# A long-attention and token-mixer kernel: the third batch is begun earlier, the v copies change engine, and TensorE gets more filler

## The chip, the cores and the metric

The kernel runs on one core of one Trainium2 chip, as one program. Five engines work beside each other, each taking its own instructions in order: TensorE (PE; its weight loads are shown as PEld), VectorE (DVE), ScalarE (ACT), GpSimd (POOL) and SyncE (SP), which does little but hand out DMA transfers. The metric is the device time of one execution in microseconds (us), the median of several. An execution's time contains the span from its first to its last instruction and a little around it.

## What is computed

Inputs are q, k and v of 8 batches, 8 heads, 576 positions and 64 dimensions, eight global positions, and four weight matrices. Attention is limited to a band of 32 positions on either side, except that the eight global positions see everything and are seen by everything. The attention output of the eight heads, side by side, is x (8 x 576 x 512). An MLP-mixer block follows, once over the positions and once over the channels:

```python
scores = scale * np.matmul(q, k.transpose(0, 1, 3, 2))
mask = (np.abs(pos[:, None] - pos[None, :]) <= 32) | is_global[:, None] | is_global[None, :]
attn = softmax(np.where(mask, scores, -1e9))
x = heads_side_by_side(np.matmul(attn, v))
u = x + (np.maximum(x.T @ w_tok1, 0.0) @ w_tok2).T
out = u + np.maximum(u @ w_ch1, 0.0) @ w_ch2
```

## The kernel before

The order of every instruction is written out by hand: an engine takes its instructions in the order in which the Python code emits them, and the framework only adds the semaphores. The work of one batch has short names in the code, which the whole text uses.

**Attention of batch b.** `load_qk` and `load_rest` (SP) fetch q and k as 32-bit numbers; `cast_qk` makes 16-bit copies, a pair of heads at a time (`casts` gives ten such steps: the rest rows and four pairs, for q and for k). `T(b, p)` turns one head pair with eight transposes on TensorE, and `TE` copies the two results on VectorE into `qT` and `kT`; `t` is both. `TR` does the same for the last 64 rows, with `TRE`. `globals_` copies the queries of the global positions into `qT` (L391). `S_(b, p, part)` computes half of a head pair's banded scores, and `SX` (ScalarE, L469) exponentiates them into `e_all`. `SM` (VectorE) picks the global queries' part into `eg` (L475) and multiplies `e_all` with the band's mask (L480). `GK` computes the scores of the global keys, with two exponentials and a mask product (`LM`, L531). `OG` (L538) multiplies `eg` with v and leaves `rf` (L543, VectorE). `PV(b, tau)` makes the output of 128 positions; VectorE divides (L677, L678) into `x16s`. `PV` needs v twice: as loaded by POOL's DMA queue (`load_v16`, five loads, into `vsh`), and shifted by 64 rows (`vod`), which `v_odd` makes with two copies of 64 x 2112 elements (L372, L373), on POOL for most batches.

**Mixer of batch b.** `M1` is the first token product (L691, five chunks, then one Relu on ScalarE, L695); `M2` the second (L711), whose sums VectorE makes (L716, L719); `M3` turns them by DMA transposes on SP's queue (L728) into `uT`. `M4(b, j)`, j from 0 to 11, is one group of the first channel product ("product 1", L739) with a Relu (L742), and `M5(b, tau, part)` half a tile of the second ("product 2", L765); after the second half VectorE adds (L769) and SP stores the tile (L770). `M4l` and the fifth tile of M5 handle the last 64 positions of two batches together, in odd b (L752, L772).

**How the two are woven.** `dense(b)` lists the units of M4 and M5 of batch b, 20 for even b and 25 for odd ones. While these run, attention of the next batches is put between them. For b=0, `period_0` is a hand-written list in which every `D` (None) stands for "the next dense unit"; `play` walks it and then emits the units that are left. For b=1, `merge` interleaves the list `sparse2()` with the dense units by the costs written beside the entries. From b=2 on, `first_half(b)` is played with product 1 and `second_half(b)` with product 2; there PV and the token product of batch b+1 and the turning and scoring of batch b+2 are placed. Since POOL has little else to do, its queue runs ahead of this order: a `load_v16` goes out as soon as the PV that last read its buffer is done.

The prologue (L883 to L1016) does the attention and token product of batch 0 by pairs of heads; `W(n)` (L205) puts n matmuls of 128 x 128 on TensorE whose result nobody reads. Its last POOL instructions load the weights, q, k and v of batch 1 and cast batch 1's q and k.

PSUM tiles come from three pools: `psS` with two slots (scores, most turned pairs, M1, M2), `psV` with one (PV of even tau, GK, OG) and `psM` with two (M4, M5, and the turned pairs of batches 0 and 2).

Of the kernel before, what the change touches and what calls it, by code (L numbers as in the profile page):

```python
# [44 lines left out]
def kernel(  # L45
# [156 lines left out]

    warm = psv([P, P], name="warm")

    def W(n):  # L205
        for _ in range(n):
            nc.tensor.matmul(warm, lhsT=ident, rhs=ident, start=True, stop=True)

    def indices():
        g16r = const.tile([1, NG], F16)  # L210
# [156 lines left out]
            nc.gpsimd.dma_start(out=dr.rearrange("p i d -> p (i d)"), in_=rest_src(ten, 1))  # L367
            nc.gpsimd.dma_start(out=dst.rearrange("p h i d -> p h (i d)"), in_=qk_src(ten, 1, slice(0, H)))

    def v_odd(b, hs=slice(0, H), eng=nc.gpsimd):  # L370
        i = b % 2
        eng.tensor_copy(out=vod[i][HQ:P, :, hs], in_=vsh[i][HQ:P, 0 : NT - 1, hs])  # L372
        eng.tensor_copy(out=vod[i][0:HQ, :, hs], in_=vsh[i][0:HQ, 1:NT, hs])  # L373
# [13 lines left out]
    def casts(b):  # L387
        return [lambda ti=ti, p=p: cast_qk(b, ti, p, nc.scalar.copy) for p in (None, 0, 1, 2, 3) for ti in range(2)]
# [53 lines left out]
    def S_(b, p, part):  # L442
        qf = qTs[b % 2][:, p].rearrange("p t x -> p (t x)")
        kT = kTs[b % 2][:, p]
        ps = pss([P, 2, 512], name=f"s{part}_{b}_{p}")
        a, z = ((0, 2 * QS), (2 * QS, ES))[part]
        if b == 0:
            for par in range(2):
                nc.tensor.matmul(ps[:, par, 0 : z - a], lhsT=ident, rhs=band[:, 0 : z - a], start=True, stop=False)
        js = ((0, 1, 2, 3, 4), (4, 5, 6, 7, 8, 9))[part]  # L450
        for j in js:
            i0 = max(qcol(j - 1), a)
            i1 = min(qcol(j) + HQ + NG * (j % 2 == 0), z)
            o = slice(HQ * (j % 2), HQ * (j % 2) + HQ)
            for par in range(2):
                r = slice(64 * par, 64 * par + 64)
                nc.tensor.matmul(  # L457
                    ps[o, par, i0 - a : i1 - a], lhsT=kT[r, HQ * j : HQ * j + HQ], rhs=qf[r, i0:i1],
                    start=b > 0, stop=b > 0 or j in js[-2:],
                )  # L460
        st[b]["s", p, part] = ps
        if b > 0:
            SX(b, p, part)
# [7 lines left out]
    def SM(b, p):  # L471
        e2 = e_all[:, 2 * p : 2 * p + 2]
        if b > 0:
            gc = bass.AP(tensor=e2.tensor, offset=e2.offset, ap=[e2.ap[0], [QS, NT], [ES, 2], [1, NG]])
            nc.vector.tensor_tensor(  # L475
                out=eg[:, :, 2 * p : 2 * p + 2, 0:NG], in0=gc, in1=egm.unsqueeze(2).to_broadcast([P, NT, 2, NG]), op=ALU.mult
            )
        bm = bandm.rearrange("p c x -> p (c x)")[:, 0:ES]
        for par in range(2):
            nc.vector.tensor_mul(out=e2[:, par], in0=e2[:, par], in1=bm)  # L480
# [26 lines left out]
    def GK(b):  # L507
        s = st[b]
        ps = (psv if b != 2 else pss)([P, 2, 512], name=f"gk_{b}")
        for p in range(NP):  # L510
            o = ps[32 * p : 32 * p + 32]
            qv = qTs[b % 2][:, p, :, NG:QS]
            w = kgz[:, b, p, :]
            nc.tensor.matmul(o[:, 0, 0:384], lhsT=w, rhs=qv[:, 0:3], start=True, stop=True)
            nc.tensor.matmul(o[:, 1, 0:128], lhsT=w, rhs=qv[:, 3], start=True, stop=True)
            nc.tensor.matmul(o[:, 1, 128:192], lhsT=w, rhs=qv[:, 4, 0:LAST], start=True, stop=True)
        s["gk"] = ps
        if b > 0:
            LX(b)
            LM(b)  # L520
# [255 lines left out]
    def t(b, p):  # L776
        T(b, p)
        TE(b, p)

    def sparse2():  # L780
        b, n = 2, 3
        cs = casts(n)

        def cast(k):
            return [(0.0, c) for c in cs[2 * k : 2 * k + 2]]

        u = [(0.0, lambda: (load_rest(n), load_qk(n, slice(0, H))))]
        for p in (2, 3):
            u += [(0.3, lambda p=p: S_(b, p, 0)), (1.8, lambda p=p: S_(b, p, 1)), (0.0, lambda p=p: SM(b, p))]
            if p == 2:  # L790
                u += [(0.3, lambda: GK(b))]
        u += [(2.5, lambda: OG(b))]
        u += [(2.0, lambda: PV(b, 0)), (2.0, lambda: PV(b, 1)), *cast(0), (2.0, lambda: PV(b, 2)), *cast(1)]
        u += [(0.0, lambda: PV(b, 3)), (1.0, lambda: [M1(b, ch) for ch in range(3)]), *cast(2)]
        u += [(2.0, lambda: PV(b, 4)), *cast(3), (3.0, lambda: [M1(b, ch) for ch in range(3, NT)]), *cast(4)]
        u += [(0.0, lambda: (load_rest(n + 1), load_qk(n + 1, slice(0, H))))]
        u += [(0.0, lambda: (load_v16(n), v_odd(n)))]
        u += [(1.3, lambda: (M2(b, 0), M3(b, 0))), (1.0, lambda: (M2(b, 1), M3(b, 1)))]
        u += [(2.0, lambda: (M2(b, 2), M3(b, 2) if b % 2 else None))]
        u += [(1.0, lambda: (globals_(n), TR(n)))]  # L800
        u += [(1.2, lambda p=p: t(n, p)) for p in range(NP)]
        for p in range(NP):
            u += [(0.3, lambda p=p: S_(n, p, 0)), (2.2, lambda p=p: S_(n, p, 1)), (0.0, lambda p=p: SM(n, p))]
            if p == 2:
                u += [(0.5, lambda: GK(n))]
        u += [(0.5, lambda: OG(n))]
        return u

# [13 lines left out]
    def period_0():  # L822
        n, m = 1, 2
        D = None
        c2 = casts(m)
        u = [D, D, D, D, D, lambda: TR(n), D, lambda: globals_(n), lambda: t(n, 0), D]
        u += [lambda: t(n, 1), D, s2(n, 0), D, lambda: t(n, 2), lambda: SM(n, 0), D, s2(n, 1), D, lambda: t(n, 3)]
        u += [lambda: SM(n, 1), s2(n, 2), D]
        u += [D, lambda: SM(n, 2), lambda: GK(n), s2(n, 3), D, lambda: SM(n, 3), D, D, D]
        u += [lambda: v_odd(n, eng=nc.vector), lambda: OG(n), D, lambda: (load_rest(m), load_qk(m, slice(0, H)))]  # L830
        u += [lambda: PV(n, 0), lambda: PV(n, 1), D, lambda: PV(n, 2), lambda: PV(n, 3), D]
        u += [lambda: PV(n, 4), lambda: [M1(n, ch) for ch in range(NT)], *c2]
        u += [lambda: (M2(n, 0), M3(n, 0)), lambda: (M2(n, 1), M3(n, 1)), lambda: globals_(m), lambda: TR(m), lambda: t(m, 0)]
        u += [lambda: (M2(n, 2), M3(n, 2)), lambda: (load_v16(m), v_odd(m)), lambda: t(m, 1), s2(m, 0), lambda: t(m, 2)]
        u += [lambda: SM(m, 0), lambda: t(m, 3), s2(m, 1), lambda: SM(m, 1)]
        return u

    def first_half(b):
        n, m = b + 1, b + 2
        D = None  # L840
        cs = casts(m) if m < B else []

        def c(k):
            return cs[2 * k : 2 * k + 2]

        def tt(p):
            return [lambda: t(m, p)] if m < B else []

        def pv(tau):
            return lambda: PV(n, tau)  # L850

        if n == B:
            return []
        u = [D, D, pv(0), D, pv(1), *c(0), D, pv(2), *c(1), D, pv(3), lambda: [M1(n, ch) for ch in range(3)], *c(2), D]
        if b == 2:
            u += [lambda: gather_t(1)]
        u += [pv(4), *([lambda: TR(m)] if m < B else []), *tt(0), *c(3), D, lambda: M1(n, 3), D, lambda: M1(n, 4), *c(4)]
        if m < B:
            u += [lambda: (load_v16(m), v_odd(m)), lambda: globals_(m)]
        if m + 1 < B:  # L860
            u += [lambda: (load_rest(m + 1), load_qk(m + 1, slice(0, H)))]
        u += [*tt(1), D, D, lambda: (M2(n, 0), M3(n, 0)), D, lambda: (M2(n, 1), M3(n, 1)), *tt(2), D]
        u += [lambda: (M2(n, 2), M3(n, 2) if n % 2 else None), D]
        return u

    def second_half(b):
        m = b + 2
        D = None
        if m >= B:
            return []  # L870
        return [D, s2(m, 0), D, lambda: t(m, 3), lambda: SM(m, 0), D, s2(m, 1), D, lambda: SM(m, 1), D, s2(m, 2), D,
                lambda: SM(m, 2), lambda: GK(m), s2(m, 3), D, lambda: SM(m, 3), D, lambda: OG(m)]

    def dense(b):
        u = [(0.86, lambda j=j: M4(b, j)) for j in range(NJ)]
# [34 lines left out]
    S_(0, 0, 0)  # L910
    TRE(0, (0,), A)
    TRE(0, (1,), V)
    S_(0, 1, 0)
    SX(0, 0, 0)
    G(out=g16[0][0], in_=g32[0][0])
    T(0, 2)
    load_w1()
    load_w1l()
    load_w2()
    SX(0, 1, 0)  # L920
    S_(0, 1, 1)
    TEk(0, 2, V)
    S_(0, 0, 1)
# [6 lines left out]
    G(out=g16[1][0], in_=g32[1][0])  # L930
    TEq(0, 3, A)
    TEk(0, 3, V)
    S_(0, 2, 0)
    castv(0)
    gather_t(0)
# [3 lines left out]
    castv(1)  # L939
    GKE(0)  # L940
    SX(0, 2, 1)
    GQ0()
    v_odd(0, slice(0, 2), nc.vector)
    v_odd(0, slice(2, 4), nc.vector)
    GK(0)
    GX0()
    S_(0, 3, 1)
# [3 lines left out]
    castv(2)  # L951
    load_wc1(0)
    SX(0, 3, 1)
    OG0(1)
    LM(0)
    OG0(0)
# [18 lines left out]
    load_v16(1)  # L975
    x_pads(1)
    qk_pads(1)
    for p in (None, 0, 1, 2, 3):
        cast_qk(1, 0, p, G)
        cast_qk(1, 1, p, G)  # L980
    gather(1)
# [76 lines left out]
```

The softmax here doesn't subtract the row's maximum and nothing guards it: scores larger than these inputs give would overflow.

## Time and profile before

| what | us |
|---|---|
| median of 7 runs | 354.27 |
| lowest and highest | 349.99, 355.27 |
| the profiled execution | 350.85 |
| its span, first to last instruction | 349.1 |
| TensorE busy | 311.4 (89% of the span) |
| VectorE busy | 189.5 (54%) |
| ScalarE busy | 153.6 (44%) |
| POOL busy | 86.7 (25%) |

Times of single instructions are from that one execution and count from the start of its span. In a timeline row stand the start, the duration, the engine, the line of the code, the operation, what it writes and reads, shape and count, and in brackets how long the engine was idle before and what ended that. "Granted clock" is the share of TensorE's full clock that the throttle let through: 1.00 or 0.50 in this trace, by stretches of 3.41 us or a multiple of it.

### The profile page before, as it was taken

How to read it: one execution, taken by the hardware profiler on the slowest of the kernel's cores; microseconds unless marked ns; L12 is line 12 of the kernel's file. 1: busy time of each engine (PE TensorE's matmuls, PEld its weight loads, DVE VectorE, ACT ScalarE, POOL GpSimd, SP SyncE). 2: the span in 40 equal slices, each digit the busy share in tenths (PEclk: the TensorE clock that was granted, in tenths of full speed). 3: DMA queues.
4: the chain of work that ended last, by engine and by line, in shares of the span. 5: the costliest groups of instructions: out<-in, count | busy, mean ns of one | idle time of the engine just before them, and what ended most of it. 6: DMA issues, size and time to landing. Idle time of an engine off the chain costs nothing.

```text
span 349.1 us, 8086 instructions
## 1 busy us (share of the span) xinstructions
PE 311.4 (89%) x3431; PEld 168.7 (48%) x3431; DVE 189.5 (54%) x395; ACT 153.6 (44%) x275; POOL 86.7 (25%) x111
## 2 busy tenths in 40 slices
PE   4599686984899989799989999899989999999993
PEld 4368343542446544454445645444545645444641
DVE  7488176845852766566656474565656364231021
ACT  2562435214858135653465453554455433413600
POOL 5948586441226000430044001520000000000000
PEclk9789989998999999999999999999999999999999
DMA  7999999199767972949294923959101221042012
GB/s 208 191 143 245 262 159 76 62 218 221 220 117 71 255 141 62 87 100 257 93 88 78 238 90 73 90 174 204 62 2 26 67 81 44 0 107 91 0 69 85
DMA packets 82023, 42.38 MB, mean 121 GB/s; under 512 B 56578, under 2 KB 76674, under 8 KB 81986
## 3 DMA queue, kind: packets, MB, share of 16 engines
q1 hardware_dynamic: 44080, 31.34, 33.7%
q0 software_dynamic: 37904, 10.52, 28.2%
q8 instruction: 27, 0.44, 0.5%
q14 instruction: 10, 0.08, 0.1%
q10 hardware_dynamic: 2, 0.00, 0.0%
HBM read 36.11 MB, written 9.44 MB: 130 GB/s over the span
## 4 chain that ended last, share of the span: by engine, by line
PE 72%; DMA 11%; issue 5%; DVE 5%; SPq 3%; POOL 2%; ACT 2%; ACTq 0%; POOLq 0%
PE op L765 25%; PE b1p L739 23%; DMA lk<-in_k_dram 9%; PE a1p L691 4%; PE s L457 4%; PE hp L711 4%; PE pT L399 3%; PE b1lp L752 3%; PE pv L655 3%; PE pv L664 2%; DMA lv<-in_v_dram 2%; DVE x L678 1%; PE og L538 1%; SPq L128 1%; SPq L126 1%
## 5 line engine op out<-in xcount | busy, mean ns | idle before, releaser
L742 ACT ACTIVATE b<-b1p 128x512 f16<-128x512 f32 x96 | 57.0, 598 | 91.5 <-PE b1p L739 89.6
L739 PE MATMUL b1p<-uT,wc 128*128 128x512 f16 x384 | 95.9, 383 | 0.5 <-ACT b L742 0.5
L765 PE MATMUL op<-wc,b 128*128 128x512 f16 x384 | 89.3, 380 | 0.0
L469 ACT ACTIVATE e_all<-s 128x544 f16<-128x544 f32 (+1 forms) x64 | 41.1, 685 | 41.2 <-issue 29.1
L360 POOL DMA_DIRECT2D vsh<-in_v_dram x35 | 29.6, 854 | 115.7 <-PE pv L664 99.2
L765 PEld LDWEIGHTS <-b 128*128 128x128 f16 x384 | 35.3, 98 | 39.4
L739 PEld LDWEIGHTS <-wc 128*128 128x128 f16 x384 | 34.6, 98 | 37.1 <-issue 1.8
L769 DVE TENSOR_TENSOR osb<-u,op 128x512 f32<-128x512 f16 x32 | 22.0, 688 | 53.9 <-PE op L765 51.7
L405 DVE COPY qT<-pT 128x512 f16<-128x512 f16 x30 | 20.6, 687 | 15.0 <-PE pT L399 11.3
L716 DVE TENSOR_TENSOR u<-x,hp 128x1024 f16<-128x1024 f16 x14 | 17.0, 1221 | 21.3 <-PE hp L711 21.3
L677 DVE RECIPROCAL rr<-pv 128x8 f32<-128x8 f32 (+1 forms) x35 | 7.2, 207 | 33.3 <-PE pv L664 33.2
L457 PE MATMUL s<-qT,kT 64*64 64x136 f16 (+2 forms) x704 | 18.6, 223 | 7.4 <-DVE kT L411 1.9
L480 DVE TENSOR_TENSOR e_all<-e_all,bandm 128x616 f16<-128x616 f16 x56 | 24.4, 476 | 1.0
L678 DVE TENSOR_TENSOR x<-pv,rr 128x512 f16<-128x512 f32 (+1 forms) x35 | 24.2, 691 | 1.2
L457 PEld LDWEIGHTS <-kT 64*64 64x64 f16 x704 | 11.9, 110 | 20.5 <-issue 13.6
L411 DVE COPY kT<-pT 128x512 f16<-128x512 f16 x30 | 20.4, 681 | 2.0 <-ACT qT L405 1.2
L399 PE MATMUL pT<-ident,qn 128*128 128x128 f16 x128 | 14.3, 242 | 7.2 <-DVE kT L437 6.3
L711 PE MATMUL hp<-a,w 128*128 128x512 f16 x72 | 18.9, 380 | 1.5 <-ACT a L695 1.5
L655 PE MATMUL pv<-rf,lf 128*64 128x264 f16 x126 | 18.9, 287 | 0.9 <-DVE kgz L354 0.7
L664 PE MATMUL pv<-vsh,e_all 128*64 128x66 f16 x280 | 18.5, 194 | 0.0
L664 PEld LDWEIGHTS <-e_all 128*64 128x64 f16 x504 | 18.4, 111 | 0.0
L385 ACT CAST qn<-lq 128x512 f16<-128x512 f32 x25 | 15.3, 613 | 6.5 <-DMA lq<-in_q_dram 6.5
(171 smaller groups left out, 368.6 us busy)
## 6 DMA issues: line engine op xcount, KB each, us to landing
out_dram<-osb SPq DMA_DIRECT2D x32, 256.0 KB
lq<-in_q_dram SPq DMA_DIRECT2D x6, 1024.0 KB
lk<-in_k_dram SPq DMA_DIRECT2D x6, 1024.0 KB
wc<-in_moe_w_ch_dram POOLq DMA_DIRECT2D x6, 512.0 KB
vsh<-in_v_dram POOLq DMA_DIRECT2D x21, 128.0 KB
vsh<-in_v_dram POOLq DMA_DIRECT2D x14, 96.0 KB
lq<-in_q_dram SPq DMA_DIRECT2D x4, 256.0 KB
lk<-in_k_dram SPq DMA_DIRECT2D x4, 256.0 KB
```

What stands on the lines that cost most here:

```text
L360: nc.gpsimd.dma_start(out=vsh[b % 2][r0:r1, c, :, 0:D], in_=v[b, :, j0 : j0 + (r1 - r0), :].rearrange("h p d -> p h d"),)
L399: nc.tensor.transpose(out=pT[:, ti, P * i : P * i + P], in_=n[b % 2][:, i, 2 * p : 2 * p + 2, :], identity=ident)
L457: nc.tensor.matmul(ps[o, par, i0 - a : i1 - a], lhsT=kT[r, HQ * j : HQ * j + HQ], rhs=qf[r, i0:i1], start=b > 0, stop=b > 0 or j in js[-2:],)
L469: nc.scalar.activation(out=e2[:, :, a:z], in_=ps[:, :, 0 : z - a], func=AF.Exp, scale=scale)
L480: nc.vector.tensor_mul(out=e2[:, par], in0=e2[:, par], in1=bm)
L655: nc.tensor.matmul(ps[r0 : r0 + 64, hf, 0 : NP * VW], lhsT=s["lf"][:, HQ * t : HQ * t + HQ], rhs=s["rf"][:, 2 * hf : 2 * hf + 2], start=Tr ...
L664: nc.tensor.matmul(ps[r0 : r0 + 64, hf, VW * hh : VW * hh + VW], lhsT=e_all[:, h, lo : lo + HQ], rhs=(vod if t % 2 else vsh)[b % 2][:, tau ...
L678: nc.vector.tensor_tensor(out=x16s[b % 2][r, tau, :].rearrange("p (f h x) -> p f h x", f=2, h=NP), in0=pq[r, :, :, 0:D], in1=rr[r].unsquee ...
L711: nc.tensor.matmul(ps[:, i, :], lhsT=w2[:, ch, P * tau - sh : P * tau - sh + P], rhs=s["a1"][:, ch, :], start=(ch == 0), stop=(ch == 1),)
L739: nc.tensor.matmul(ps, lhsT=wc1[:, cc, P * j : P * j + P], rhs=s["uT"][:, cc, :], start=(cc == 0), stop=(cc == 3))
L742: nc.scalar.activation(out=s["b1"][:, j, :], in_=ps, func=AF.Relu)
L765: nc.tensor.matmul(ps, lhsT=w, rhs=wc2[:, j, :], start=(j == 0), stop=(j == NJ - 1))
```

## The change

- `W` may take a fresh tile from `psM`. Seven calls with 74 matmuls together are added in the prologue: 30 before the scores of the second head pair, 12 before the turn of the third, five of 4 or 16 further on.
- POOL casts only the rest rows and pairs 0 and 1 of batch 1 in the prologue. Pairs 2 and 3 are cast by ScalarE in `period_0`.
- `period_0` is written anew: six instead of five dense units before `TR(1)`; the gk product of batch 1 and its last scores with a dense unit between; the loads of batch 2 after the 15th unit, ahead of `SM(1, 3)`; the v copies of batch 1 after that `SM`; the last unit before the last chunk of M1. Nine casts of batch 2 on ScalarE, and the tenth (pair 3 of k) on POOL, right before `load_v16(2)`. At the end the scores of batch 2's pair 2 with their `SM`, which were in `sparse2`.
- `sparse2` begins with `GK(2)` and pair 3, then the v copies.
- `v_odd` runs on VectorE for every batch. It leaves `period_0`'s tail and `first_half` and stands after `GK` in `sparse2` and `second_half`.

```diff
-    def W(n):
+    def W(n, fresh=False):
+        w = psm([P, P], name="warm2") if fresh else warm
         for _ in range(n):
-            nc.tensor.matmul(warm, lhsT=ident, rhs=ident, start=True, stop=True)
+            nc.tensor.matmul(w, lhsT=ident, rhs=ident, start=True, stop=True)
...
-    def v_odd(b, hs=slice(0, H), eng=nc.gpsimd):
+    def v_odd(b, hs=slice(0, H), eng=nc.vector):
...
         u = [(0.0, lambda: (load_rest(n), load_qk(n, slice(0, H))))]
-        for p in (2, 3):
-            u += [(0.3, lambda p=p: S_(b, p, 0)), (1.8, lambda p=p: S_(b, p, 1)), (0.0, lambda p=p: SM(b, p))]
-            if p == 2:
-                u += [(0.3, lambda: GK(b))]
+        u += [(0.3, lambda: GK(b)), (0.3, lambda: S_(b, 3, 0)), (1.8, lambda: S_(b, 3, 1)), (0.0, lambda: SM(b, 3))]
+        u += [(0.0, lambda: v_odd(b))]
         u += [(2.5, lambda: OG(b))]
...
-        u += [(0.0, lambda: (load_v16(n), v_odd(n)))]
+        u += [(0.0, lambda: load_v16(n))]
...
-                u += [(0.5, lambda: GK(n))]
+                u += [(0.5, lambda: GK(n)), (0.0, lambda: v_odd(n))]
...
-        c2 = casts(m)
-        u = [D, D, D, D, D, lambda: TR(n), D, lambda: globals_(n), lambda: t(n, 0), D]
-        u += [lambda: t(n, 1), D, s2(n, 0), D, lambda: t(n, 2), lambda: SM(n, 0), D, s2(n, 1), D, lambda: t(n, 3)]
-        u += [lambda: SM(n, 1), s2(n, 2), D]
-        u += [D, lambda: SM(n, 2), lambda: GK(n), s2(n, 3), D, lambda: SM(n, 3), D, D, D]
-        u += [lambda: v_odd(n, eng=nc.vector), lambda: OG(n), D, lambda: (load_rest(m), load_qk(m, slice(0, H)))]
+        c2 = casts(m)[:-1]
+        c1 = [lambda ti=ti, p=p: cast_qk(1, ti, p, nc.scalar.copy) for p in (2, 3) for ti in range(2)]
+        u = [D, D, D, D, D, D, lambda: TR(n), lambda: globals_(n), D, lambda: t(n, 0), *c1[:2], D]
+        u += [lambda: t(n, 1), *c1[2:], D, s2(n, 0), D, lambda: t(n, 2), lambda: SM(n, 0), D, s2(n, 1), D]
+        u += [lambda: t(n, 3), lambda: SM(n, 1), s2(n, 2), D, lambda: SM(n, 2), lambda: GK(n), D, s2(n, 3), D]
+        u += [lambda: (load_rest(m), load_qk(m, slice(0, H))), lambda: SM(n, 3), lambda: v_odd(n), D, lambda: OG(n), D]
         u += [lambda: PV(n, 0), lambda: PV(n, 1), D, lambda: PV(n, 2), lambda: PV(n, 3), D]
-        u += [lambda: PV(n, 4), lambda: [M1(n, ch) for ch in range(NT)], *c2]
+        u += [lambda: PV(n, 4), lambda: [M1(n, ch) for ch in range(NT - 1)], D, lambda: M1(n, NT - 1), *c2, D]
+        u += [lambda: (cast_qk(m, 1, 3, G), load_v16(m))]
         u += [lambda: (M2(n, 0), M3(n, 0)), lambda: (M2(n, 1), M3(n, 1)), lambda: globals_(m), lambda: TR(m), lambda: t(m, 0)]
-        u += [lambda: (M2(n, 2), M3(n, 2)), lambda: (load_v16(m), v_odd(m)), lambda: t(m, 1), s2(m, 0), lambda: t(m, 2)]
-        u += [lambda: SM(m, 0), lambda: t(m, 3), s2(m, 1), lambda: SM(m, 1)]
+        u += [lambda: (M2(n, 2), M3(n, 2)), lambda: t(m, 1), s2(m, 0), lambda: t(m, 2)]
+        u += [lambda: SM(m, 0), lambda: t(m, 3), s2(m, 1), lambda: SM(m, 1), s2(m, 2), lambda: SM(m, 2)]
...
-            u += [lambda: (load_v16(m), v_odd(m)), lambda: globals_(m)]
+            u += [lambda: load_v16(m), lambda: globals_(m)]
...
-                lambda: SM(m, 2), lambda: GK(m), s2(m, 3), D, lambda: SM(m, 3), D, lambda: OG(m)]
+                lambda: SM(m, 2), lambda: GK(m), lambda: v_odd(m), s2(m, 3), D, lambda: SM(m, 3), D, lambda: OG(m)]
...
     S_(0, 0, 0)
     TRE(0, (0,), A)
     TRE(0, (1,), V)
+    W(30)
     S_(0, 1, 0)
     SX(0, 0, 0)
     G(out=g16[0][0], in_=g32[0][0])
+    W(12)
     T(0, 2)
...
     SX(0, 3, 1)
+    W(16, True)
     OG0(1)
...
-    for p in (None, 0, 1, 2, 3):
+    for p in (None, 0, 1):
         cast_qk(1, 0, p, G)
         cast_qk(1, 1, p, G)
```

(Left out: four further calls of `W(4)`, before `S_(0, 1, 1)`, `S_(0, 2, 0)`, `GQ0()` and `GK(0)`.)

More of the change, by code (lines that the diff above doesn't have):

```diff
@@ L824, in period_0 @@
         D = None
-        c2 = casts(m)
-        u = [D, D, D, D, D, lambda: TR(n), D, lambda: globals_(n), lambda: t(n, 0), D]
-        u += [lambda: t(n, 1), D, s2(n, 0), D, lambda: t(n, 2), lambda: SM(n, 0), D, s2(n, 1), D, lambda: t(n, 3)]
-        u += [lambda: SM(n, 1), s2(n, 2), D]
-        u += [D, lambda: SM(n, 2), lambda: GK(n), s2(n, 3), D, lambda: SM(n, 3), D, D, D]
-        u += [lambda: v_odd(n, eng=nc.vector), lambda: OG(n), D, lambda: (load_rest(m), load_qk(m, slice(0, H)))]
+        c2 = casts(m)[:-1]
[4 more added lines that the diff above has]
+        u += [lambda: (load_rest(m), load_qk(m, slice(0, H))), lambda: SM(n, 3), lambda: v_odd(n), D, lambda: OG(n), D]
         u += [lambda: PV(n, 0), lambda: PV(n, 1), D, lambda: PV(n, 2), lambda: PV(n, 3), D]
-        u += [lambda: PV(n, 4), lambda: [M1(n, ch) for ch in range(NT)], *c2]
+        u += [lambda: PV(n, 4), lambda: [M1(n, ch) for ch in range(NT - 1)], D, lambda: M1(n, NT - 1), *c2, D]
+        u += [lambda: (cast_qk(m, 1, 3, G), load_v16(m))]
         u += [lambda: (M2(n, 0), M3(n, 0)), lambda: (M2(n, 1), M3(n, 1)), lambda: globals_(m), lambda: TR(m), lambda: t(m, 0)]
-        u += [lambda: (M2(n, 2), M3(n, 2)), lambda: (load_v16(m), v_odd(m)), lambda: t(m, 1), s2(m, 0), lambda: t(m, 2)]
-        u += [lambda: SM(m, 0), lambda: t(m, 3), s2(m, 1), lambda: SM(m, 1)]
+        u += [lambda: (M2(n, 2), M3(n, 2)), lambda: t(m, 1), s2(m, 0), lambda: t(m, 2)]
+        u += [lambda: SM(m, 0), lambda: t(m, 3), s2(m, 1), lambda: SM(m, 1), s2(m, 2), lambda: SM(m, 2)]
+        return u
         return u
@@ L920 @@
     SX(0, 1, 0)
+    W(4)
     S_(0, 1, 1)
@@ L932 @@
     TEk(0, 3, V)
+    W(4)
     S_(0, 2, 0)
@@ L941 @@
     SX(0, 2, 1)
+    W(4)
     GQ0()
@@ L944 @@
     v_odd(0, slice(2, 4), nc.vector)
+    W(4)
     GK(0)
```

## The prediction

> **What bounds the kernel now.** First the slices of the page, where every digit is the busy tenth of one fortieth of the span (8.7 us).
>
> ```profile
> PE   4599686984899989799989999899989999999993
> DVE  7488176845852766566656474565656364231021
> POOL 5948586441226000430044001520000000000000
> PEclk9789989998999999999999999999999999999999
> ```
>
> After about 95 us TensorE is full; what an edit can win lies in the first eleven slices. Second, the chain that ended last, for what paces those slices (start, us, what).
>
> ```profile
> 28.29 12.77 DMA lk<-in_k_dram
> 41.34 0.79 POOL vsh L360
> 42.17 0.52 POOL x L295
> ...
> 69.70 0.65 SPq L120
> 70.46 0.60 SPq L120
> 71.73 12.26 DMA lk<-in_k_dram
> 84.02 0.63 ACT kn L385
> ```
>
> Until 43 us the end hangs on batch 1's k and on POOL, not on TensorE. At 70 us it hangs on batch 2's k, which SP asks for only after an output store (L769, L770) has let it go. Third, the timeline of TensorE, whose brackets give each idle stretch.
>
> ```profile
> 43.09 0.32 PE L426 MATMUL pr<-ident,qr 128*64 128x64 f16 x8 [2.76 <-POOL qr L382]
> ...
> 55.17 0.34 PE L457 MATMUL s<-qT,kT 64*64 64x72 f16 x12 [1.94 <-DVE kT L411]
> ...
> 77.76 1.89 PE L711 MATMUL hp<-a,w 128*128 128x512 f16 x8 [1.48 <-ACT a L695]
> ...
> 84.69 0.40 PE L399 MATMUL pT<-ident,kn 128*128 128x128 f16 x4 [3.88 <-ACT kn L385]
> ```
>
> With the small ones (0.88, 0.79, 0.39, 0.28, 0.63, 0.47, 0.16) the idle time between 43 and 97 us is about 14 us. Fourth, VectorE beside POOL:
>
> ```profile
> 44.47 3.45 DVE L391 COPY qT<-gT 128x160 f16<-128x160 f16 x1
> ...
> 66.26 0.71 DVE L372 COPY vod<-vsh 64x2112 f16<-64x2112 f16 x1
> 67.00 0.70 DVE L373 COPY vod<-vsh 64x2112 f16<-64x2112 f16 x1
> ```
>
> The globals copy takes 0.20 us at 81.09, with POOL idle; here it ends just when POOL's casts do (47.86). The v copies of one batch cost VectorE 1.41 us; on POOL they took 1.94 and 2.06.
>
> **Prologue filler.** 74 more 128x128 matmuls. Twenty of them took 2.05 us of weight loads at 5.72, 0.103 each, so 7.6 us at half clock and, halving, an estimated 3.8 at full. 1.9 us fills the idle before the second head pair's scores (14.98). Nothing on POOL waits for TensorE there: its loads and casts keep their times, and the turn of batch 1's rest rows stays at 43.1. Against that TensorE has 2.76 us to spare, of which the sixth M4 group (0.86), now ahead of it, uses one part; 1.9 is left. Here the clock:
>
> ```profile
> 13.61:17.02 3.41, 2.04 (x28) 1.36 (x32) 1.71 (x4) 1.90 (x4) 3.41 (x7) 0.50 0.99 169
> 17.02:20.44 3.42, 3.42 (x49) 2.04 (x48) 2.21 (x5) 2.15 (x4) 0.69 (x2) 0.50 1.19 184
> 40.92:44.33 3.41, 1.21 (x19) 0.72 (x20) 0.54 (x2) 0.04 (x1) 2.95 (x6) 1.00 1.24 206
> 44.33:47.74 3.41, 3.41 (x18) 2.00 (x17) 3.41 (x2) 0.77 (x2) 3.41 (x7) 0.50 1.43 194
> ```
>
> The columns are stretch, length, busy us of PE, PEld, DVE, ACT, POOL, granted clock, DMA. A stretch 60% busy is followed by half clock when it was at half itself, one 35% busy by half clock. The Trainium skill (TensorE: Matmul & The Clock Gate, "Why this matters for your kernels") asks only that idle gaps stay below about 3 us. By that rule the 2.76 us gap costs nothing and this filler nothing but its price; by the rows it cost 3.4 us at half, in which 1.7 us of matmul time was lost. I go by the rows: 30 fillers make 13.61-17.02 full, so 17.02-20.44 runs at full, and wins back up to 1.7 of the 3.8; with ScalarE and VectorE now next there, TensorE reaches the M4 groups about 2 us later (bounds: 0.5 earlier to 4 later). All but 0.2 of it is inside the spare 1.9, and it leaves 40.92-44.33 over 70% busy, so the next stretch at full. **+0.2** (0 to 2.2).
>
> **Casts of batch 1.** Four of POOL's (0.56 pitch each) go to ScalarE, which stood idle 4.05 us there (ACT at 45.01): free. POOL's block then ends at 45.6, and L391 with it, so the first turn's copies start at 45.65 instead of 47.83. Walked on: second turn at 46.0, its copies to 48.2, where the second score part can start, against 50.36. The third pair's copies follow their turn (before they started at 53.83, 1.7 us after their turn's end, which no row of their own explains), so the 1.94 becomes 0.4; the 0.79 stays. Group thirteen starts at 54.4, where before group twelve started at 58.24: 3.84 plus its 0.87 is **-4.7** (the sixth group's move is in it). At half clock the same walk gives 55.7, -3.4.
>
> **v copies of batch 1** are on VectorE in both, but now come straight after SM(3) and ahead of rf: score end +1.4 (Exp) +1.1 (SM) +1.4 +0.7, and one store add 0.7, is 5.2, while TensorE comes to PV(0) at +4.3 to +4.6. **+0.6** (0 to 1.0). So M2 starts at 73.7, before 77.76.
>
> **Order inside product 2.** PV, OG, gk and M1 keep their durations; one M5 unit now stands before M1's last chunk, where before there was no wait (a gap of 0.15 or more is not in the timeline), so nothing. The list has 21 places for 20 dense units: the last, after the casts, stays empty, and the 1.48 before M2 with it.
>
> **Loads of batch 2** go out behind the first store, not the third: about 61 instead of 69.7. At the old 12.3 us k lands by 73 to 75, before ScalarE is through the token Relu; the POOL loads of v that shared the queues then (69.34 on) now come later. The last k pair's cast moves to POOL, idle then, which takes 0.5 off ScalarE's ten casts; they were not last in the tail. So the 3.88 and 0.39 go. Then VectorE is next: from M2's start, 1.06 to its first output, adds 2.35, globals and rest 1.0, that is to +4.2; the first pair's two copies to +5.4, ul's add +6.0, second pair +7.2, third +8.4, SM(0) +9.5, fourth pair +10.7, SM(1) and SM(2) to +12.9 (0.6 per copy, 1.1 per SM). Before, the first copy could start at +7.4 only. TensorE follows it: scores of pair 1 at +8.7, of pair 2 when ScalarE has freed their tiles, +9.5 to +10.4, gk to +11.6, and then the first M4 of batch 1; before that came at +12.75, with pair 2 and gk left over. uT's transposes, issued at +2.3 in four steps of 1.5, land near +10: no wait, if barely. Then two M4 instead of four before OG, one 0.7 wait for eg, the v copies ahead of rf: PV(0) of batch 2 at +17.7 with four M4 done; before +20.95 with six. 3.25 minus 2x0.87 is **-1.5** (-3 to +0.5).
>
> **v copies on VectorE** in each later batch (3 to 7). They sit between LM and SM(3), and eg, e_all, the store add, rf and OG queue behind. In the sparse stretch OG waits for eg already:
>
> ```profile
> 134.20 0.69 DVE L772 TENSOR_TENSOR osb<-ul,op 128x512 f32<-128x512 f16 x1 [0.55 <-PE op L765]
> 134.81 0.19 DVE L475 TENSOR_TENSOR eg<-e_all,egm 128x80 f16<-128x80 f16 x1
> ```
>
> The 0.55 idle before the store add, less the Exp rows that still come in it, hides 0.4 of the 1.41: OG comes 1.0 later. In the play-ordered periods eg was ready at 170.64 and OG started at 171.47; with the copies eg is ready at 171.74 (+0.3), and the store add, then rf, cost another 0.2 where no M5 follows: 2x0.5, and 2x0.25 in odd periods with their fifth tile. **+2.5** (0 to 7.0, all five uncovered). What comes back: L391 at 150.27 and 185.57 falls from 1.47 and 1.70 to 0.20. The Trainium skill (SBUF — State Buffer, "Who interferes with whom") says that copies on the port pair that VectorE and GpSimd share exclude each other for a whole instruction. By it alone the move gives VectorE about what it costs (1.3 against 1.41); but the idle row before TE at 151.99 shows nobody waiting for L391, so it gives the end nothing. I take nothing.
>
> **Sum.** 0.2-4.7+0.6-1.5+2.5 = -2.9 on the profiled execution: 349.1 span plus 1.75 around it, 350.85 to 348.0. That execution lies 3.4 below the median of its seven runs, which spread from 350 to 355. Nothing shown says why; I read it as throttled stretches that fall elsewhere in other runs, each worth up to 1.7, and let filler and denser units spare 1.0 of it, an estimate. 354.27-2.9-1.0 = **350.4**.
>
> **Rivals.** (1) Half clock stays at 44.33 and the copies lose another microsecond: the sum is -2.9+1.3+1.0, the spared 1.0 doesn't come: 353.7. For it: only 45% busy if the prologue doesn't slip. 0.38, nearly all within 1%.
> (2) Slower: batch 2's v comes too late. Its five loads, which POOL gave out at 52.89 before, now queue there behind the cast of the last k pair, and that waits for k. VectorE's v copy of batch 2 waits for them, with SM's successors, rf and every store add queued behind it, and OG reads the same rows. Alone the five took 7.7 us from first issue to landing (52.89 to 60.62); batch 3's, beside q and k traffic, took 16.5 (69.34 to 85.82). With k at 74 the first goes out at 74.7 and v lands between 82.4 and 91.2; the copies are due at 89.4 (M2's start +15.7). If batch 3's v, next in the same queue, and the transposes stretch it by another lone 7.7 it is 98.9: 9.5 us of stall, all of it on the path, 350.4+9.5 = 359.9. It turns the change into a loss once v lands after 93.3. Against it: q and k are asked for 8.7 us earlier into quiet queues. 0.14.
> (3) The whole 3.4 between median and profile goes with the throttled stretches, and the tail wins 3.0: 354.27-2.9-1.5-3.4 = 346.5. For it: two of the seven runs were without it already. 0.10.
> The forecast has 0.38.
>
> A measurement tells this kernel from no change at about 1% (3.5 us). Faster by more: all of (3) and 0.32 of the forecast, which lies just below that line with more room downwards (tail, filler), 0.42; slower 0.14; the rest 0.44. The range 346.0 to 357.0 takes in the bounds of tail and copies, and leaves out (2) and a little of (3).
>
> **To see afterwards.** L391 near 1.2 at 45 and 0.20 elsewhere; full clock from 20 to 48; SP's batch 2 loads near 61; no wait for kn L385 near 84, but waits for DVE in 74-90; OG behind eg by 0.3 to 1.0 from 134 on. Wrong if VectorE waits for vsh, if the turn of batch 1 moves past 44, or if each OG waits a full 1.4.

## The result, and the profile after

| what | before | after |
|---|---|---|
| median, us | 352.94 (62 runs) | 353.23 (25 runs) |
| lowest to highest | 348.60 to 358.14 | 350.23 to 356.75 |
| profiled span | 349.1 | 350.7 |
| granted clock over the span | 0.979 | 0.971 |

The ratio of after to before is 1.0049, with a 95% interval of 1.0024 to 1.0074: half a per cent slower, about 1.7 us, where 1.1% faster was forecast. Here and below a ratio compares runs on the same chip and leaves out the disturbed ones, which the medians contain, so the two can differ, in one case by 0.9%.

The slices of the changed kernel:

```profile
PE   5788998976799998799989999899989999999993
DVE  7477756849442866566655475565756384241021
POOL 5795640073031001300040001200000000000000
PEclk9989999996599999999999999999999999999998
```

TensorE is denser in slices 1, 2, 5 to 7 and 10 and thinner in 3, 4, 9 and 11, and POOL's busy time fell from 25% to 18% of the span. But the clock now has its dip in slices 10 and 11 (half clock from 81.5 to 95.2 us), deeper than any before. Next the timeline of TensorE, with the stalls that answer to those shown before. Line numbers are one higher than in the kernel before.

```profile
45.07 0.32 PE L427 MATMUL pr<-ident,qr 128*64 128x64 f16 x8
...
64.72 0.30 PE L656 MATMUL pv<-rf,lf 128*64 128x264 f16 x2 [0.60 <-DVE rf L544]
...
75.09 1.89 PE L712 MATMUL hp<-a,w 128*128 128x512 f16 x8 [1.17 <-ACT a L696]
...
90.04 1.87 PE L740 MATMUL b1p<-uT,wc 128*128 128x512 f16 x4 [3.29 <-DMA uT<-u]
...
134.94 0.46 PE L539 MATMUL og<-vsh,eg 128*32 128x132 f16 x17 [1.55 <-DVE eg L476]
```

The 2.76 and the 3.88 of before are gone. In their place stands a wait of 3.29 for uT, the transposed input of product 1 of batch 1. M2 of batch 1 comes 2.67 us earlier than before (75.09 against 77.76), but the first M4 group only 0.47 earlier (90.04 against 90.51), and its four matmuls take 1.87 instead of 1.04: half clock. The chain that ended last goes through the transposes:

```profile
80.51 0.70 DVE ul L720
81.21 0.27 SPq L729
81.48 0.05 issue
81.53 8.38 DMA uT<-u
89.91 0.14 issue
90.04 1.87 PE b1p L740 x4
```

The last of the four transposes is issued at 81.53 and lands 8.4 us later. What ran beside it is in POOL's timeline:

```profile
72.55 0.61 POOL L386 CAST kn<-lk 128x512 f16<-128x512 f32 x1 [22.32 <-DMA lk<-in_k_dram]
73.15 8.49 POOL L361 DMA_DIRECT2D vsh<-in_v_dram  x10
```

The cast of batch 2's last k pair held POOL's queue for 22 us. Behind it stood the v loads of batch 2, which had gone out at 52.89 before, and right after those went batch 3's: ten loads in one block, just where SP issues the transposes. In the 8.4 us from the last issue to the landing, 4399 packets of POOL's queue went through the DMA engines beside 2363 of SP's, and all but 64 of the 4399 before 87.0.

### The profile page after: what moved, and what is told of

Same layout as the page of the kernel before. It is cut to its first block, busy times and chain, and to the rows that moved or that the text cites. A ratio compares the mean times of both kernels' runs of the same rounds, so it can differ in the third digit from the quotient of the medians.

```text
span 350.7 us, 8246 instructions
## 1 busy us (share of the span) xinstructions
PE 317.0 (90%) x3505; PEld 172.8 (49%) x3505; DVE 193.8 (55%) x407; ACT 155.1 (44%) x278; POOL 61.4 (18%) x96
## 4 chain that ended last, share of the span: by engine, by line
PE 75%; DVE 16%; issue 4%; DMA 2%; ACT 1%; SPq 0%; DVEq 0%; ACTq 0%
PE b1p L740 24%; PE op L766 22%; PE a1p L692 5%; PE hp L712 4%; PE pv L656 3%; PE s L458 3%; PE b1lp L753 3%; PE pT L400 3%; PE pv L665 2%; DMA uT<-u 2%; DVE osb L770 1%; DVE vod L373 1%; DVE vod L374 1%; DVE qT L406 1%; DVE kT L412 1%
## 5 line engine op out<-in xcount | busy, mean ns | idle before, releaser
L770 DVE TENSOR_TENSOR osb<-u,op 128x512 f32<-128x512 f16 x32 | 21.9, 686 | 56.0 <-PE op L766 54.0
L400 PE MATMUL pT<-ident,qn 128*128 128x128 f16 x128 | 13.3, 230 | 8.7 <-DVE kT L438 7.4
L386 ACT CAST qn<-lq 128x512 f16<-128x512 f32 x27 | 16.5, 613 | 3.3 <-DMA lq<-in_q_dram 3.3
```

The source lines that it names most:

```text
L770: nc.vector.tensor_add(out=osb, in0=s["u16"][:, tau], in1=ps)
```

## The experiments

Each edit is made to the changed kernel, unless the text names another start. Each was timed beside the kernel before on the same chip; that kernel's median was 353.57 beside the first four, 352.64 beside the next four, 351.21 beside the last three. The changed kernel was not timed again beside them: what an edit gains on it is read from the traces, or roughly from its ratio set against 1.0049.

**Batch 2's v loads early.** One pair of steps is exchanged:

```diff
-        u += [lambda: (cast_qk(m, 1, 3, G), load_v16(m))]
+        u += [lambda: (load_v16(m), cast_qk(m, 1, 3, G))]
```

> The changed kernel, but on POOL's queue batch 2's five v loads stand ahead of the cast of its last k pair instead of behind it, so they go out near 51 us again; nothing else moves. Theory A (the DMA transposes of uT land late because both batches' v loads run beside them): the last transpose lands 3 to 8 us after its issue less than the 8.4 us seen, the first M4 group of batch 1 starts near 87 instead of 90.0, the 3.3 us wait of TensorE for uT goes below 0.5, and at least one of the four half-clock stretches behind it goes: 349 to 350 us median, 3 to 5 us below the changed kernel. Theory B (the transposes are slow by themselves, or the tail is held by VectorE alone): the wait stays above 2.5 us and the time within 1 us of the changed kernel.

347.99 us, ratio 0.9845 (0.9803 to 0.9886). Its timelines of POOL, then of TensorE:

```profile
50.52 4.34 POOL L361 DMA_DIRECT2D vsh<-in_v_dram  x5
70.83 0.61 POOL L386 CAST kn<-lk 128x512 f16<-128x512 f32 x1 [15.97 <-DMA lk<-in_k_dram]
71.38 4.20 POOL L361 DMA_DIRECT2D vsh<-in_v_dram  x5
```

```profile
84.49 1.89 PE L740 MATMUL b1p<-uT,wc 128*128 128x512 f16 x4
```

The wait for uT is gone. The first M4 group stands 11.6 us after M2 (72.90), where it was 14.95. Of the 5.5 us by which this span (345.2) is shorter than the changed kernel's, 3.4 are this; 2.2 were there at M2 already, and they are the prologue's, which differs from one execution to the next (see the filler). Theory A holds, theory B falls; the median came out below the 349 to 350 that theory A named. Two half-clock stretches of 3.41 us remain instead of four.

**The v copies back on POOL**, for batches 3 to 7:

```diff
-        u += [(0.0, lambda: load_v16(n))]
+        u += [(0.0, lambda: (load_v16(n), v_odd(n, eng=nc.gpsimd)))]
...
-                u += [(0.5, lambda: GK(n)), (0.0, lambda: v_odd(n))]
+                u += [(0.5, lambda: GK(n))]
...
-            u += [lambda: load_v16(m), lambda: globals_(m)]
+            u += [lambda: (load_v16(m), v_odd(m, eng=nc.gpsimd)), lambda: globals_(m)]
...
-                lambda: SM(m, 2), lambda: GK(m), lambda: v_odd(m), s2(m, 3), D, lambda: SM(m, 3), D, lambda: OG(m)]
+                lambda: SM(m, 2), lambda: GK(m), s2(m, 3), D, lambda: SM(m, 3), D, lambda: OG(m)]
```

> The changed kernel with the v copies of batches 3 to 7 back on POOL in their old places; batch 1's and 2's stay on VectorE. Theory A (the copies sit in VectorE's chain ahead of eg and rf): the wait of OG for eg at 134.9 falls from 1.55 to about 0.7, the drift of 1.8 us between 135 us and the end goes, and the time is 2.4 to 2.8 us below the changed kernel. Theory B (POOL's copies cost as much through the lock on VectorE's SBUF copies): less than 0.7 us.

349.48 us, ratio 0.9880 (0.9835 to 0.9926). Its timeline of TensorE:

```profile
89.52 1.87 PE L740 MATMUL b1p<-uT,wc 128*128 128x512 f16 x4 [4.19 <-DMA uT<-u]
...
133.57 0.46 PE L539 MATMUL og<-vsh,eg 128*32 128x132 f16 x17 [0.72 <-DVE eg L476]
```

The wait of OG is 0.72 again. From the first OG matmul of batch 3 to the end it takes 214.9 us, the changed kernel 217.6, the kernel before 215.0. So the copies cost 2.6 to 2.7 us at their places, and the wait for uT is not theirs: it is still there. The time fell by more than theory A's 2.4 to 2.8 (3.8 in the medians, more by the ratios); what is above the 2.7 lies ahead of batch 3's OG and is not explained.

**No filler**: the seven new calls of `W` are left out.

```diff
-    W(30)
...
-    W(12)
...
-    W(16, True)
```

> The changed kernel without the 74 added filler matmuls of the prologue. Theory A (the filler makes the prologue 4 us longer, of which 2 reach the turn of batch 1's rest rows at 45.1, and in return keeps full clock at 44 to 48): the turn is back at 43.1, a half-clock stretch follows it, and the gk product comes within 1 us of the changed kernel; time within 1 us of it. Theory B (the filler is only a cost): 2 us faster. Theory C (the filler pays beyond its price, also in other runs): 2 us slower or more.

353.24 us, ratio 0.9899 (0.984 to 0.9958); the six runs spread from 349.19 to 356.26. In the profiled one the first M4 group starts at 36.35 (changed kernel: 39.76) and the turn of batch 1's rest rows at 42.16 (45.07). But between 44 and 80 us that execution had no half-clock stretch either, and POOL was earlier by itself in it. So theory A's second half is not shown, and with this spread the median doesn't tell the three apart. The ratio, 1.5% below the changed kernel's, speaks for theory B, but it rests on three of the six runs; the filler alone, further down, does not bear it out. TensorE's wait for uT is in this execution too: 2.92 us.

**Early v loads and copies on POOL together**: the first two edits.

> The first two edits together: batch 2's v loads ahead of the cast, and the copies of batches 3 to 7 on POOL. Theory A: the two gains are at different places and add up, 5 to 8 us below the changed kernel, 346 to 348 us, and so below the kernel before too. Theory B (one of them only shifts the wait to the next limit): not more than the better of the two alone, within 0.7 us.

347.00 us, ratio 0.9771 (0.9725 to 0.9817): within the 346 to 348 that theory A gave, and below the kernel before. In the median that is 1.0 below the better of the two, not the sum. Its profiled execution lost the prologue: half clock from 21.2 to 28.0, so that its first M4 group starts at 41.09 and M2 at 76.99, against 37.14 and 72.90 with early v loads alone; from OG of batch 3 on it is 2.6 us shorter than that one, as expected. That the gains add up at their places is shown; that they add up in the time is not.

**Only batch 3's v loads out of the way**: a copy of one element of uT stands ahead of them on POOL, and holds them until uT has landed. The copy's output is read by nobody.

```diff
-        u += [(0.0, lambda: load_v16(n))]
+        u += [(0.0, lambda: (nc.gpsimd.tensor_copy(out=seen, in_=st[1]["uT"][0:1, 0, 511:512]), load_v16(n)))]
```

> The changed kernel, with batch 3's five v loads held back on POOL until uT of batch 1 has landed (a copy of one element of uT stands ahead of them); batch 2's v loads stay where the change put them, beside the transposes. It halves the traffic beside the transposes instead of moving it away. Theory A (the transposes are late in proportion to what shares the DMA engines): the last one lands 3 to 6 us after its issue instead of 8.4, TensorE's wait for uT falls from 3.3 to between 0 and 1.5 us, the time to 349 to 351 us. Theory B (it is batch 2's loads alone, by their place right ahead of the transposes): wait above 2.5 us, time within 1 us of the changed kernel.

347.02 us, ratio 0.9857 (0.9795 to 0.9918). The copy is also a clock for the landing. POOL's timeline:

```profile
72.71 4.33 POOL L362 DMA_DIRECT2D vsh<-in_v_dram  x5
83.06 0.48 POOL L797 COPY seen<-uT 1x1 f16<-1x1 f16 x1 [6.02 <-DMA uT<-u]
83.60 4.20 POOL L362 DMA_DIRECT2D vsh<-in_v_dram  x5
```

The last transpose, issued at 80.48, had landed by 83.06: 2.6 us, not 8.4, although batch 2's five loads went out right ahead of the transposes. The first M4 group is at M2 + 11.6 again. So theory B falls, and the landing is below theory A's 3 to 6. The five loads were nearly through by then: after 80.48 only 41 packets of POOL's queue passed, where the changed kernel had 4399. So this run does not show what five loads cost a transpose that they really run beside, nor whether the cost is in proportion; it shows that with batch 3's five away TensorE doesn't wait. SP's loads of q and k for batch 3 are no rival: they go out 2.7 us after the last transpose in this run and 2.8 in the changed kernel, and here uT has landed by then.

**The filler alone, in the kernel before**: the seven calls.

```diff
+    W(30)
...
+    W(12)
...
+    W(16, True)
```

> The kernel before with the 74 filler matmuls of the change and nothing else. Theory A (the filler pushes the prologue behind POOL's casts, and gives back what it costs as full clock at 44 to 48): the turn of batch 1's rest rows 0 to 3 us later than 43.1, no half-clock stretch after it, time within 1 us of the kernel before. Theory B (only a cost): 2 us slower. Theory C (it steadies the clock of the prologue in other runs): 1 to 2 us faster in the median, with a narrower spread.

351.74 us (22 runs), ratio 1.0010 (0.9978 to 1.0043). Theory A's size holds: no gain, no cost. The turn came at 42.30 in the profiled execution, earlier than in the kernel before, since POOL was, and full clock held from 14.6 to 79. Theories B and C fall, and the spread (348.2 to 354.9) is hardly narrower.

**Reordered.** On top of both edits: the dense unit behind the casts, and batch 2's v copies on ScalarE.

```diff
+    def odd_act(b):
+        i = b % 2
+        nc.scalar.copy(out=vod[i][HQ:P], in_=vsh[i][HQ:P, 0 : NT - 1])
+        nc.scalar.copy(out=vod[i][0:HQ], in_=vsh[i][0:HQ, 1:NT])
...
+        u += [lambda: (load_v16(m), odd_act(m))]
         u += [lambda: PV(n, 0), lambda: PV(n, 1), D, lambda: PV(n, 2), lambda: PV(n, 3), D]
-        u += [lambda: PV(n, 4), lambda: [M1(n, ch) for ch in range(NT - 1)], D, lambda: M1(n, NT - 1), *c2, D]
+        u += [lambda: PV(n, 4), lambda: [M1(n, ch) for ch in range(NT)], *c2, D]
...
-        u += [lambda: (load_v16(m), cast_qk(m, 1, 3, G))]
+        u += [lambda: cast_qk(m, 1, 3, G)]
...
-        u += [(0.0, lambda: v_odd(b))]
```

> The combined kernel (batch 2's v loads early, copies of batches 3 to 7 on POOL) with two more moves: the dense unit that the change put ahead of M1's last chunk stands behind the casts, where the list has a place without a unit, and batch 2's two v copies are made by ScalarE while it is idle near 61 to 73 us instead of by VectorE ahead of rf. Expected: TensorE's wait of 1.17 us ahead of M2 is filled, with none new ahead of M1's last chunk; the 0.7 us wait of PV for rf in batch 2 falls below 0.2: 1.2 to 2.2 us below the combined kernel, 345 to 346 us. Rival: VectorE sets the pace from M2 on, and what is won ahead of it is lost in its chain: within 0.7 us of the combined kernel.

347.24 us, ratio 0.9871 (0.9796 to 0.9946): nothing gained on the kernel that it starts from, which had 0.9771 on another chip. The 1.17 ahead of M2 and the 0.7 ahead of PV are filled as expected, but a new wait of 2.88 us stands at the gk product. VectorE, then POOL:

```profile
82.15 1.70 DVE L481 TENSOR_TENSOR eg<-e_all,egm 128x80 f16<-128x80 f16 x1
83.89 2.64 DVE L486 TENSOR_TENSOR e_all<-e_all,bandm 128x616 f16<-128x616 f16 x2
```

```profile
81.86 1.95 POOL L373 COPY vod<-vsh 64x2112 f16<-64x2112 f16 x1 [4.78 <-DMA vsh<-in_v_dram]
83.86 1.94 POOL L374 COPY vod<-vsh 64x2112 f16<-64x2112 f16 x1
```

POOL's v copies for batch 3 fall into VectorE's densest stretch. A product of 0.20 us, and a pair of products that together take 0.87, last 1.70 and 2.64 us beside POOL's two copies. Here POOL's copies are the dearer ones; that POOL is the cheaper place holds for the later periods only.

**The idle stretch of the prologue filled**, in the reordered kernel: a `W(16)`, 16 more matmuls, ahead of the turn of batch 0's last pair.

```diff
+    W(16)
```

> The kernel of the run before it with 16 more filler matmuls right ahead of the turn of batch 0's last head pair, where TensorE waited about 1.4 us for VectorE's casts in every profile of the changed kind. Theory A (that idle stretch is what drops the prologue to half clock): the half-clock stretches between 20 and 28 us go, the first M4 group starts at 36 to 38 us instead of up to 41, the spread narrows, and the median falls by 1 to 2 us. Theory B (the phase of the clock stretches decides): no change beyond 0.7 us.

347.71 us, ratio 0.9882 (0.9809 to 0.9955). The first M4 group starts at 38.22, and no stretch below full is left between 20 and 28 us; but in the profiled run before it that was so as well. The median doesn't move and the spread stays. Theory A is not supported.

**Batch 3's v held back** in the reordered kernel, by the same one-element copy.

```diff
+        u += [(0.0, lambda: nc.gpsimd.tensor_copy(out=seen, in_=st[1]["uT"][0:1, 0, 511:512]))]
```

> The reordered combined kernel (unit behind the casts, batch 2's copies on ScalarE, batches 3 to 7 on POOL), with batch 3's v loads, and so its POOL copies, held back until uT of batch 1 has landed. In that kernel POOL copied batch 3's v at 81.9 to 85.8, and a product of e_all and the mask on VectorE took 2.25 us instead of 0.48. Theory A (that lock delays VectorE's chain and the first M4 group of batch 1): the group starts 11.6 us after M2 instead of 14.2, the wait of 2.9 us at the gk product goes, 1.5 to 2.6 us less: 344 to 346 us. Theory B (the wait only moves on): within 0.7 us.

343.94 us, ratio 0.9782 (0.9718 to 0.9846), 3.3 below the kernel that it starts from in the median, on another chip; the intervals of the two ratios overlap. VectorE at the place of the two rows above:

```profile
80.40 0.20 DVE L482 TENSOR_TENSOR eg<-e_all,egm 128x80 f16<-128x80 f16 x1
80.63 0.87 DVE L487 TENSOR_TENSOR e_all<-e_all,bandm 128x616 f16<-128x616 f16 x2
```

The group starts 11.6 us after M2, and the wait at the gk product is gone. Theory A holds at its place; the size in the time is not shown so closely. No v load runs beside the transposes here: the last, issued at 78.03, had landed by 80.57, after 2.5 us.

**The v copies alone, in the kernel before**: batches 3 to 7 on VectorE in the places of the change.

```diff
-        u += [(0.0, lambda: (load_v16(n), v_odd(n)))]
+        u += [(0.0, lambda: load_v16(n))]
...
-                u += [(0.5, lambda: GK(n))]
+                u += [(0.5, lambda: GK(n)), (0.0, lambda: v_odd(n))]
...
-            u += [lambda: (load_v16(m), v_odd(m)), lambda: globals_(m)]
+            u += [lambda: load_v16(m), lambda: globals_(m)]
```

> The kernel before with the v copies of batches 3 to 7 on VectorE in the places of the change, and nothing else. Theory A (they cost TensorE what was read between 133 us and the end of the changed kernel): 2.4 to 2.8 us slower than the kernel before, all of it after 130 us, in the waits of OG for eg and of the first M4 groups. Theory B (what POOL's copies cost through the lock is won back): within 1 us.

353.41 against 351.21 us, 2.2 apart; the ratio is 1.0076 (1.0049 to 1.0104), that is 2.7 us. OG's wait in batch 3 is 1.55 in its timeline, and from there to the end it takes 217.6 us, to a tenth what the changed kernel takes. Theory A holds.

**Filler in the tail of period_0**: 46 matmuls where TensorE waits for VectorE, on top of the held v.

```diff
+    def WT(n):
+        w = psv([P, P], name="warm3")
+        for _ in range(n):
+            nc.tensor.matmul(w, lhsT=ident, rhs=ident, start=True, stop=True)
...
-        u += [lambda: (M2(n, 2), M3(n, 2)), lambda: t(m, 1), s2(m, 0), lambda: t(m, 2)]
-        u += [lambda: SM(m, 0), lambda: t(m, 3), s2(m, 1), lambda: SM(m, 1), s2(m, 2), lambda: SM(m, 2)]
+        u += [lambda: (M2(n, 2), M3(n, 2)), lambda: WT(16), lambda: t(m, 1), lambda: WT(10), s2(m, 0), lambda: WT(6), lambda: t(m, 2)]
+        u += [lambda: SM(m, 0), lambda: t(m, 3), lambda: WT(8), s2(m, 1), lambda: SM(m, 1), lambda: WT(6), s2(m, 2), lambda: SM(m, 2)]
```

> The kernel with the held v loads, with 46 filler matmuls of 128 x 128 in the places between M2 of batch 1 and pair 2's scores of batch 2 where TensorE waited for VectorE (16, 10, 6, 8 and 6 of them). Theory A (that idle stretch throttles the clock, and the throttled stretches reach into the M4 groups behind it): the two half-clock stretches from about 80 to 87 us go, 0.7 to 2 us less than without the filler. Theory B (TensorE waits there anyway, the clock costs nothing): within 0.5 us. Theory C (the filler lies on the path): slower.

343.06 us, ratio 0.9755 (0.9691 to 0.9819): the fastest of all, 8.2 us below the kernel before on that chip. The granted clock in the page's slices, first with the v held, then with the filler too:

```profile
PEclk9999999996999999899999999999999999999999
```

```profile
PEclk9999999999999999999999999999999999999999
```

The stretch ahead of the dip, first with the v held, then at the same distance from M2 with the filler too (columns as in the prediction):

```profile
75.66:79.08 3.42, 1.82 (x38) 1.34 (x38) 3.36 (x6) 1.61 (x3) 0.00 (x0) 1.00 0.51 98
```

```profile
75.31:78.72 3.41, 2.80 (x58) 2.32 (x56) 3.35 (x6) 1.60 (x3) 0.00 (x0) 1.00 0.52 102
```

In the profiled executions the first M4 group of batch 1 comes at M2 + 11.1 instead of 11.6, and from there to the twelfth group it takes 16.3 us instead of 17.1, since the clock stays full. In the medians the gain is 0.9, with overlapping intervals: shown for the place, not for the time.

## Why the prediction was wrong

The mechanism that failed is one clause of the tail: "uT's transposes, issued at +2.3 in four steps of 1.5, land near +10: no wait, if barely". They were issued as said (77.40 is M2 + 2.3, the fourth at +6.4) and landed at +14.8. The step counted what the moved v loads do to v, not what they do to the other queue. The second rival held that very move, named its place behind the cast, and asked only whether v would be late; VectorE never waited for v in the changed kernel. The Trainium skill says under DMA: Bandwidth & Descriptors, "Queues, rings and completion order", that an engine takes turns between its queues packet by packet. The trace agrees as far as it goes: from 81.53 to 87.0 us, 4335 packets of POOL's queue and 1241 of SP's went through side by side. The size is shown by the runs alone: 8.4 us from issue to landing with ten v loads in flight, 2.6 with five that were nearly through (batch 3's v held), 2.5 with none (the reordered kernel with v held).

By the prediction's own terms, on the profiled executions:

- **Filler, +0.2.** TensorE reached the M4 groups about 4 us later (39.76 for 35.80), the end of the bounds that were given, not 2. Full clock held from 44 to 48 as said, but half clock moved to 20.1 to 23.5. The turn came 1.8 later than the sum had it. In the medians the filler is worth nothing either way (1.0010).
- **Casts, -4.7.** From the turn to group thirteen the walk had 11.3 us (43.1 to 54.4); 10.9 were measured (45.07 to 55.97). The globals copy (L391 before) took 0.19 at 47.05, with POOL's casts ended; the predicted 1.2 was wrong for the late turn.
- **v copies of batch 1, +0.6.** Measured 0.60. M2 was put at 73.9 with the filler's 0.2, and came at 75.09, 1.2 late: 1.8 from the prologue, less what the walk won.
- **Tail, -1.5.** The waits for q and k went, and VectorE's chain ended where it was put (SM(2) at +13.1 for +12.9). With the v loads early, the first M4 group stands at +11.59, where +11.6 was said. In the changed kernel it stood at +14.95, and PV of batch 2 at +21.9 instead of +17.7: 3.3 of the 4.2 are the wait, the rest half clock, which reached to 95.2.
- **v copies on VectorE, +2.5.** 2.6 measured, from both sides. The bound below, nothing, and the bound above, 7.0, were far off. As the prediction had it, the globals copy fell to 0.20 and 0.19 (at 150.15 and 186.02), and gave the end nothing.
- **The 1.0 to be spared** between median and profile can't be made out: the medians moved by 0.3 and the profiled executions by 1.7, but the ratio gives 1.7 as well. Nor were there fewer half-clock stretches in the profiled execution, five against four before up to 100 us. Four of the five follow each other here:

```profile
78.11:81.52 3.41, 1.41 (x32) 0.89 (x30) 3.35 (x8) 1.73 (x4) 3.41 (x5) 1.00 2.21 149
81.52:84.94 3.42, 2.82 (x51) 2.23 (x48) 3.27 (x7) 1.58 (x4) 0.12 (x1) 0.50 2.20 153
84.94:88.35 3.41, 1.53 (x34) 0.95 (x33) 3.34 (x10) 2.51 (x5) 0.00 (x0) 0.50 2.17 172
88.35:91.76 3.41, 1.72 (x4) 0.43 (x4) 0.27 (x1) 0.00 (x0) 0.00 (x0) 0.50 0.77 145
91.76:95.18 3.42, 3.42 (x48) 1.56 (x48) 1.39 (x4) 2.35 (x4) 0.00 (x0) 0.50 1.10 316
```

TensorE was busy 41% of the first stretch, and half clock followed. It ended after the one stretch in which TensorE was busy throughout; 82% at 81.52 had not been enough. With the v loads early, where TensorE doesn't wait for uT, half clock ended after two stretches.

Together: -2.9, +1.2 (prologue), +4.2 (tail), +0.1 (copies), and -0.9 that no step had (two waits in the sparse stretch, 0.48 and 0.78, became one of 0.38), is +1.7. The spans differ by 1.67. That the sum closes so well is in part luck, since the prologue's 1.2 belongs to this one execution. Luck, too, is how near the first rival's 353.7 comes to the median of 353.23: its reason, half clock at 44.33, did not occur. The largest part of what the forecast lost is a wait that it had looked at and passed.

What stays open is why executions of one kernel spread by up to 9.5 us (the kernel before). The place of the clock stretches in the prologue is part of it (first M4 group from 35.8 to 41.1 in the profiles); two kinds of filler there moved no median.

## What to carry to other kernels

When a load is moved behind a wait on its queue, ask not only who waits for that load, but what else will be on the DMA engines at its new time. Here it was four transposes between two stages, on the path that ended last. A cast that waits for a DMA does not belong ahead of loads that have nothing to wait for, on a queue taken in order. And a copy moved from an idle engine to one in the chain costs what the chain can't hide, 2.6 us here for five times 1.41; whether the idle engine is the better place depends on what the other one does in those microseconds.

## What the runs showed of the hardware

- DMA transposes beside ten v loads: 8.4 us from the last issue to landing in the changed kernel, 9.3 with the copies on POOL, 7.5 without the filler. With five v loads that were nearly through it took 2.6, with none 2.5.
- In the reordered kernel POOL's two v copies, from SBUF to SBUF, stretched a VectorE product of two SBUF operands from 0.20 to 1.70 us, and a pair of them from 0.87 to 2.64.
- A stretch of 3.41 us in which TensorE was busy 41% was followed by half clock in the changed kernel, and one at 53% (1.82 us of 3.42) in the reordered kernel with v held. With the 46 filler matmuls that stretch was 82% busy (2.80 of 3.41), and the clock stayed full. But the busy share alone doesn't settle it: in the run with early v loads and copies on POOL together, 54% (1.83 of 3.42 from 79.18) was followed by full clock.
- ScalarE makes a v copy of 64 x 2112 in 1.95 us, as long as POOL. VectorE's instructions beside it kept their lengths in the reordered kernel (v copies of batch 1 in 0.71 and 0.70).
